# A conformer block: loads of the second batch's keys spread evenly over two query chunks, parked convolution chunks fetched one every second tick

## The chip, the cores and the metric

The kernel runs on one core of a Trainium2 chip. The metric is the device time of one execution in microseconds (us). The kernel is already tuned: TensorE is busy in 99% of the span.

## The reference, cut to what matters

```python
B, T, D = 2, 4000, 512
x1 = x + 0.5 * (silu(ln(x) @ w_ff1_a) @ w_ff1_b)
q, k, v = ln(x1) @ w_q, ln(x1) @ w_k, ln(x1) @ w_v
x2 = x1 + softmax(q @ k.T * D**-0.5) @ v @ w_o
a, b = split(ln(x2) @ w_pw1)                  # pointwise product ahead of the convolution
dc = depthwise_conv(a * sigmoid(b), taps=3)   # then normalised over all tokens
x3 = x2 + silu(norm(dc)) @ w_pw2
x4 = ln(x3 + 0.5 * (silu(ln(x3) @ w_ff2_a) @ w_ff2_b))
```

## The kernel before

Attention runs in 16 query chunks `g` (8 per batch element, 508 queries each, the last of a batch 444). A chunk has 32 ticks `kt`, one per tile of 128 keys. A tick is eight matmuls (four for the scores of the tile, four that weigh the values) and what a hook adds.

The keys of one batch element fill the buffers: `h` holds them as tokens by features, `hT` transposed. The second batch's keys may overwrite tile k once chunk 7 has used tile k, and chunk 8 needs it at its tick k.

```python
# attention(), at the end of every tick; KT = 32 key tiles, TCB = 8 chunks per batch
if not self.any_score:
    if g == TCB - 1 and kt >= 6:
        self.key_tile(1, kt - 6)
    if g == TCB and kt < 6:
        self.key_tile(1, KT - 6 + kt)
hook(g, kt)
self.tick()                       # runs jobs that were put off by so many ticks

def key_tile(self, b, kt):
    ...
    self.load(self.h[kt], src, [self.b_h[kt]], reads=rd)                  # plain load, issued by SP
    self.transpose(self.hT[kc][:, kj], src, rd, [self.b_hT[kc][kj]])      # transposing load, issued by SP
```

Convolution work of the chunk before is woven into attention. When the outputs of chunk g - 1 are projected, its tokens are normalised (VectorE), each of the four tiles is transposed by a transfer that SP issues as well (at ticks 16 and 17), and at tick 22 the pointwise product reads the four transposed tiles:

```python
def att_hook(g, kt):
    ...
    if kt in (22, 27) and (0 <= g - 1 < tail or ...):
        pair(g - 1, (22, 27).index(kt))            # conv_b: product with Wp1 (in "wff"), then conv_a
    ...
    if g == NCK - 1:                               # the last chunk, 15
        if kt >= 8 and kt % 4 == 0:
            for t in (kt // 4 - 2, TCB + kt // 4 - 2):
                if t < self.NBESIDE:
                    self.fetch_conv(t)             # a parked convolution chunk, 508 KB, back from HBM
```

Key loads, query tiles, those transposes, and stores of convolution chunks (`dcvd`) all pass through SP's queue one after the other (in the recorded profile two transposes whose input was ready by 955.4 us went out from 958.18, behind a key's transposing load that held SP for 1.19 us from 956.89).

## Time and profile before

| | |
|---|---|
| first three runs | 2052.74, 2054.47, 2055.17 us |
| the recorded profile's own run | 2051.23 us, span 2047.4 us |
| TensorE busy | 2029.9 us, 17.5 us idle |
| of it in chunk 7 | 3.50 us, one wait |
| of it in chunk 15 | 0.37 us, one wait |

The lines of the profile stand in the prediction below.

### The profile page before, as it was taken

How to read it: one execution, taken by the hardware profiler on the slowest of the kernel's cores; microseconds unless marked ns; L12 is line 12 of the kernel's file. 1: busy time of each engine (PE TensorE's matmuls, PEld its weight loads, DVE VectorE, ACT ScalarE, POOL GpSimd, SP SyncE). 2: the span in 40 equal slices, each digit the busy share in tenths (PEclk: the TensorE clock that was granted, in tenths of full speed). 3: DMA queues.
4: the chain of work that ended last, by engine and by line, in shares of the span. 5: the costliest groups of instructions: out<-in, count | busy, mean ns of one | idle time of the engine just before them, and what ended most of it. 6: DMA issues, size and time to landing. Idle time of an engine off the chain costs nothing.

```text
span 2047.4 us, 24513 instructions
## 1 busy us (share of the span) xinstructions
PE 2029.9 (99%) x9647; PEld 1028.7 (50%) x9649; DVE 1092.7 (53%) x2264; ACT 744.9 (36%) x1274; POOL 109.7 (5%) x236
## 2 busy tenths in 40 slices
PE   9999999999999999999999999999999999999998
PEld 5555555554444444444444444444445555555555
DVE  4244443334556667666766676667674434434434
ACT  3433333333333333333333333333345443433433
POOL 1000000000000000000000000000011000000000
PEclk9999999999999999999999999999999999999999
DMA  8222245420101011104411111011143111111111
GB/s 182 54 62 62 53 100 125 96 70 8 26 16 31 22 31 26 30 24 108 113 34 23 26 29 32 23 26 29 42 135 93 31 31 42 31 31 42 26 36 38
DMA packets 253120, 104.41 MB, mean 51 GB/s; under 512 B 193412, under 2 KB 252487, under 8 KB 252999
## 3 DMA queue, kind: packets, MB, share of 16 engines
q1 hardware_dynamic: 252751, 102.61, 21.2%
q8 instruction: 78, 1.28, 0.3%
q14 instruction: 43, 0.35, 0.1%
q10 hardware_dynamic: 248, 0.18, 0.0%
HBM read 33.77 MB, written 23.34 MB: 28 GB/s over the span
## 4 chain that ended last, share of the span: by engine, by line
PE 97%; DVE 1%; DMA 0%; SPq 0%; issue 0%; POOL 0%; ACT 0%; POOLq 0%; DVEq 0%; ACTq 0%
PE s L500 55%; PE y L500 42%; DVE wff L1176 0%; SPq L558 0%; DVE work L612 0%; DMA work<-work 0%; DMA wff<-in_w_ff_a_dram 0%; DVE xt L753 0%; SPq L562 0%; DVE work L634 0%; POOL work L726 0%; POOL work L1185 0%; ACT work L550 0%; DVE work L547 0%; SPq L554 0%
## 5 line engine op out<-in xcount | busy, mean ns | idle before, releaser
L550 ACT ACTIVATE work<-s 128x508 bf16<-128x508 f32 (+3 forms) x1060 | 622.8, 588 | 1211.9 <-PE s L500 1208.3
L500 PE MATMUL s<-work,wff 128*128 128x508 bf16 (+5 forms) x2624 | 628.3, 371 | 6.4 <-issue 3.5
L500 PE MATMUL s<-work,keys 128*128 128x508 bf16 (+1 forms) x2048 | 516.8, 374 | 0.1
L500 PE MATMUL y<-work,keys 128*128 128x508 bf16 (+2 forms) x2048 | 504.2, 373 | 0.4 <-DVE work L999 0.4
L500 PE MATMUL y<-wff,work 128*127 128x512 bf16 x1992 | 501.2, 379 | 0.0
L920 DVE TENSOR_TENSOR work<-work 128x508 f32<-128x508 f32 (+2 forms) x496 | 334.5, 674 | 279.8 <-ACT work L550 278.6
L500 PEld LDWEIGHTS s<-work,wff 128*128 128x128 bf16 x2624 | 252.2, 98 | 283.1 <-issue 10.1
L500 PEld LDWEIGHTS y<-wff,work 128*127 128x127 bf16 x1992 | 273.7, 137 | 171.4
L500 PEld LDWEIGHTS s<-work,keys 128*128 128x128 bf16 x2048 | 199.5, 98 | 231.9 <-issue 0.6
L500 PEld LDWEIGHTS y<-work,keys 128*128 128x128 bf16 (+1 forms) x2048 | 193.5, 97 | 234.0 <-issue 6.2
L753 DVE SCALAR_TENSOR_TENSOR xt<-y,xt 127x512 bf16<-127x512 f32 x126 | 78.5, 683 | 360.5 <-PE y L500 360.5
L612 DVE BATCH_NORM_STATS2 work<-xt 127x6 f32<-127x512 bf16 x312 | 197.2, 680 | 5.9 <-DMA xt<-in_x_dram 5.8
L500 PE MATMUL s<-work 128*127 128x512 bf16 (+3 forms) x776 | 197.0, 378 | 2.2 <-DVE work L1292 1.2
L621 POOL TENSOR_TENSOR work<-work 127x4 f32<-127x4 f32 (+1 forms) x76 | 76.7, 1009 | 1133.6 <-DVE work L619 1133.6
L500 PEld LDWEIGHTS s<-work 128*127 128x127 bf16 (+1 forms) x776 | 94.9, 124 | 77.0 <-issue 3.8
L634 DVE TENSOR_SCALAR work<-xt,work 127x512 bf16<-127x512 bf16 x307 | 110.7, 406 | 26.2 <-POOL work L621 23.0
L753 DVE SCALAR_TENSOR_TENSOR xt<-s,xt 127x512 bf16<-127x512 f32 x55 | 38.0, 692 | 144.6 <-PE s L500 144.6
L753 DVE SCALAR_TENSOR_TENSOR xt<-s,work,xt 127x512 bf16<-127x512 f32 x64 | 48.0, 750 | 30.8 <-PE s L500 30.2
L1074 DVE SCALAR_TENSOR_TENSOR wff<-wff,s 128x508 bf16<-128x508 f32 (+1 forms) x57 | 38.7, 678 | 45.3 <-PE s L500 45.1
L550 ACT ACTIVATE wff<-s 128x508 f32<-128x508 f32 (+1 forms) x67 | 39.5, 591 | 58.7 <-PE s L500 58.7
L550 ACT ACTIVATE work<-keys,work 128x508 bf16<-128x508 bf16 (+1 forms) x68 | 52.2, 774 | 1.4 <-DVE work L1190 1.3
L1155 POOL COPY wff<-wff 128x1 bf16<-128x1 bf16 x56 | 10.5, 188 | 638.8 <-DVE wff L1074 636.4
(83 smaller groups left out, 424.0 us busy)
## 6 DMA issues: line engine op xcount, KB each, us to landing
keys<-keysd SPq DMA_DIRECT2D x62, 128.0 KB, 2.3
keysd<-work SPq DMA_DIRECT2D x14, 448.0 KB, 3.2
out_dram<-work SPq DMA_DIRECT2D x14, 448.0 KB, 3.2
dcvd<-wff SPq DMA_DIRECT2D x48, 127.0 KB, 1.8
keys<-dcvd SPq DMA_DIRECT2D x12, 508.0 KB, 5.1
xt<-in_x_dram SPq DMA_DIRECT2D x13, 448.0 KB, 4.9
wff<-in_w_ff_a_dram SPq DMA_DIRECT2D x16, 256.0 KB, 6.3
work<-work SPq DMA_TRANSPOSE x208, 2.5
```

Of the source, the lines that this page charges most:

```text
L500: self.S.op("PE", lambda e: e.matmul(out, lhsT, rhs, start=start, stop=stop, **kw), reads=reads, writes=[bank], inc=stop if inc is None el ...
L550: return self.S.op("ACT", lambda e: e.activation(out, in_, func, **kw), reads=reads, writes=writes)
L612: self.S.op("DVE", lambda e: e.bn_stats(self.st[sl][:, ti, :], x), reads=[b_x], writes=[self.b_st[sl][ti]])
L621: S.op("POOL", lambda e: e.tensor_tensor(out=self.rs[sl][:, 0:n], in0=self.va[sl][:, 0:n], in1=self.neghalf[0:TILE, 0:n], op=ALU.pow), rea ...
L634: self.S.op("DVE", lambda e: e.tensor_scalar(out, x, self.mv[sl][:, ti, 0:1], self.rs[sl][:, ti:ti + 1], ALU.subtract, ALU.mult), reads=[b ...
L753: self.S.op("DVE", lambda e: e.scalar_tensor_tensor(out=self.XT[g][rows], in0=ps[rows], scalar=scalar, in1=self.XT[g][rows], op0=ALU.mult, ...
L920: S.op("DVE", lambda e, p=p, n=n, acc=acc: e.tensor_tensor(out=acc, in0=acc, in1=self.P[p][0:n, 0:W], op=ALU.add), reads=[self.b_P[p], sel ...
L1074: self.S.op("DVE", lambda e: e.scalar_tensor_tensor(out=out, in0=th, scalar=1.0, in1=ps[:, 0:W], op0=ALU.add, op1=ALU.mult), reads=[b_ps, ...
L1155: S.op("POOL", lambda e: e.tensor_copy(self.G[gs][:, jj, 0:1], self.G[gp][:, jj, CHUNK:CHUNK + 1]), reads=[self.b_G[gp][jj]], writes=[self ...
```

## The change

Its intent is to relieve the SP queue where it is fullest. Keys go out over both chunks that can take them, 32 keys in 52 ticks in place of 32; parked chunks go out singly in place of in pairs.

```diff
-                if not self.any_score:
-                    if g == TCB - 1 and kt >= 6:
-                        self.key_tile(1, kt - 6)
-                    if g == TCB and kt < 6:
-                        self.key_tile(1, KT - 6 + kt)
+                if not self.any_score and TCB - 1 <= g <= TCB:
+                    at = (g - TCB + 1) * KT + kt
+                    for k in range(KT):
+                        if 6 + k * (2 * KT - 12) // KT == at:
+                            self.key_tile(1, k)
...
-                if kt >= 8 and kt % 4 == 0:
-                    for t in (kt // 4 - 2, TCB + kt // 4 - 2):
-                        if t < self.NBESIDE:
-                            self.fetch_conv(t)
+                if kt >= 8 and kt % 2 == 0:
+                    t = kt // 4 - 2 + kt // 2 % 2 * TCB
+                    if t < self.NBESIDE:
+                        self.fetch_conv(t)
```

## The prediction

> **What bounds the kernel now.** I read the page top down: engine shares first, then the chain that ended last, then busy time per stretch, and only then single instructions. The first two say that TensorE is the bound all the way through.
>
> ```profile
> PE 2029.9 (99%) x9647; PEld 1028.7 (50%) x9649; DVE 1092.7 (53%) x2264; ACT 744.9 (36%) x1274; POOL 109.7 (5%) x236
> ...
> PE 97%; DVE 1%; DMA 0%; SPq 0%; issue 0%; POOL 0%; ACT 0%; POOLq 0%; DVEq 0%; ACTq 0%
> ```
>
> TensorE is busy 2029.9 us of 2047.4. All other engines together can give back at most the 17.5 us in which TensorE did nothing, and the change touches neither its instructions nor those of VectorE, ScalarE or GpSimd: set side by side, the two builds differ in order only on the SP queue, which issues the transfers. So I looked for the part of the 17.5 us that lies where the change works. It works in two stretches of attention: the last query chunk of the first batch and the first of the second (chunks 7 and 8), and the last chunk (15). I found the chunk borders in the chain in order of time, and asked for busy time in chunks 6, 7, 8, 9, then 14 and 15 (columns: stretch, length, busy us of each engine, clock, DMA share, GB/s):
>
> ```profile
> 857.00:924.50 67.50, 67.50 (x325) 31.46 (x322) 45.01 (x77) 23.21 (x41) 2.24 (x9) 1.00 0.12 28
> 924.50:990.10 65.60, 62.10 (x323) 31.37 (x322) 43.72 (x79) 21.91 (x41) 2.24 (x9) 1.00 0.52 119
> 990.10:1058.20 68.10, 68.10 (x337) 31.55 (x337) 45.02 (x77) 23.19 (x41) 2.31 (x11) 1.00 0.27 64
> 1058.20:1126.20 68.00, 68.00 (x341) 31.90 (x338) 44.79 (x77) 23.36 (x41) 1.90 (x9) 1.00 0.12 27
> 1399.50:1466.90 67.40, 67.40 (x321) 31.34 (x322) 45.89 (x81) 23.12 (x41) 2.23 (x9) 1.00 0.12 28
> 1466.90:1518.00 51.10, 50.73 (x268) 26.23 (x265) 39.72 (x88) 17.99 (x34) 2.29 (x7) 1.00 0.45 129
> ```
>
> The reader sees full stretches (busy equals length) everywhere but two: chunk 7 lost 65.60 - 62.10 = 3.50 us, and chunk 15 lost 51.10 - 50.73 = 0.37 us. Those are the two places that the change addresses, and together they are a fifth of all idle time of TensorE. The rest (start, and the convolution's tail after 1518 us) is out of its reach.
>
> **What the 3.5 us wait for.** The timeline of TensorE and of the SP queue around it:
>
> ```profile
> 962.56 0.91 PE L500 MATMUL y<-work,keys 128*128 128x444 bf16 x4
> 966.97 0.81 PE L500 MATMUL s<-work,wff 128*128 128x508 bf16 x3 [3.50 <-issue]
> ```
>
> ```profile
> 956.26 0.58 SPq L554 DMA_DIRECT2D keys<-keysd  x1
> 956.89 1.19 SPq L558 DMA_TRANSPOSE keys<-keysd  x1
> 958.18 2.89 SPq L558 DMA_TRANSPOSE work<-work  x2
> 961.12 0.57 SPq L554 DMA_DIRECT2D keys<-keysd  x1
> 961.74 1.19 SPq L558 DMA_TRANSPOSE keys<-keysd  x1
> 963.03 2.52 SPq L558 DMA_TRANSPOSE work<-work  x2
> ```
>
> The matmuls at 966.97 are the pointwise product that opens the convolution (they read wff, the convolution weights). They need four transposed tiles of normalised tokens: the four "work<-work" transposes. The page calls the releaser "issue", that is, it saw none; but the query on the transposes of this stretch lists "PE s L500: 3.5, 1" under those who waited for them, and the fourth is issued near 964.3 us and lands about 2.6 us later, which is 966.9. Their input was ready long before: VectorE's normalisations ran at 953.38 and 954.64 us, 0.73 us each pair, so done by 955.4. The transposes sat on the SP queue behind key loads. From 942 us on that queue shows no gap: each key costs it 0.58 + 1.19 us plus gaps, 1.86 us from key to key (950.70, 952.55, 954.41, 956.26), while a tick of this narrow chunk (444 columns, 8 matmuls) takes TensorE 1.50 us. One key per tick is more than the queue can issue, so it fell behind.
>
> [...] transposes whose inputs were ready at 955.4 stood behind key loads until 965.5. [...] a transpose holds SP for a median of 1.19 us against a landing time of 2.8 us, and in chunk 7 the issuing, not the DMA engines (52% busy), is what ran out. [...] the trace has four in 0.75 us, the same with DMA at 52% as in the quiet chunk 15; so transfer traffic does not slow TensorE, and only stalls can be won.
>
> **The change, part by part.** It adds and removes no work: the same 32 keys (a plain load and a transposing load each) and 13 parked chunks.
>
> *Keys.* Before, key k is queued at tick 6 + k of chunk 7. After, at tick 6 + 1.625 k rounded down, counted over both chunks' 64 ticks: 16 keys in each chunk. The transposes for the convolution are queued at ticks 16 and 17 of the chunk, the product at tick 22. Ahead of the first pair stood keys 0 to 10, eleven of them; now keys 0 to 6, seven. Four keys less are 4 x 1.86 = 7.4 us less on SP, so the queue is through its keys at 958.1 - 7.4, about 951, and idles until the normalisations. Then I estimate: first transpose at about 953.8 (its input), second ends at 956.3, one key between the pairs as before (to 958.1), the third to 959.4, the fourth issued at 959.4 and landed 2.6 us later: 962.0. TensorE would arrive at 962.56 + 4 x 0.1875 = 963.31. The wait vanishes with some 1.3 us to spare. Worth: next start 966.97 instead of 963.31, **3.66 us** (the 3.50 of the page plus the pipeline's overlap).
>
> *Chunk 8, which receives 16 keys in place of 6.* Its ticks are about 2.1 us, a key comes every 1.625 ticks, 3.4 us, against 1.86 us of queue: no backlog. The four transposes there ran from 1022.42 to 1027.54, the last issued at 1026.26; one key between them moves it to 1028.1, landed by 1031, while the product starts at 1033.38. Key 31 is queued at tick 24, wanted at tick 31, some 15 us later, against 5 us to issue and land: no wait. The query tiles for chunk 9 were issued late, 1008.19 to 1013.3, by the old backlog; they get earlier. Cost 0.
>
> *Parked chunks.* Two every fourth tick become one every second. Five instead of six precede chunk 15's transposes, but SP had nothing to do between 1493.2 and the first transpose at 1496.20: that one waited for VectorE (normalisation at 1495.76). The fourth lands about 1502.6 as before, so this 0.37 us stays. Later ones (last fetched at tick 28 in both) are wanted only in the tail. Worth: 0, at most 0.2.
>
> *Sum:* 2054.47 - 3.66 = **2050.8 us**, a ratio of 0.998.
>
> **Rivals.** (1) The transfers are hidden anyway: time unchanged at 2054.5. For it: 97% of the chain is TensorE. Against it: the 3.50 us in chunk 7 are TensorE's own idle time, and no later slack exists to swallow them, as chunks 8 to 14 are full. (2) A new wait replaces the old: keys arriving late for chunk 8, since the last has 7 ticks of lead instead of 25, or SP blocked in order behind a store that waits for VectorE (the list of SP waits has "SPq L567 <- DVE wff L1112", longest 13.9 us). A late key could cost a few us, giving 2054 to 2058. Against it: in chunk 8 such stores are queued near ticks 7, 12 and 27, the first two far from the need of any key and the third after the last key. (3) The transposes still land late, because landing times reach 3.9 us in this stretch: the margin of 1.3 us would turn into a remainder of at most 1 us, 2051.8. (4) Bunched transfers slow matmuls, and smoothing them wins more: then chunk 7 and 15 would show wider spacing than quiet chunks. They do not.
>
> **Range and chances.** The three runs of before span 2.4 us, and its profiled run gave 2051.23, so chance alone moves a median by some 1 to 1.5 us. The mechanism puts the gain between 2.5 and 4.2 us; with run noise on both sides that makes 2048.5 to 2053.5. Faster by over 2% would need 41 us, more than twice all TensorE idle time; slower by 2% would need a stall that nothing here feeds. So 0.99 for the same.
>
> **What would show it.** Right: chunk 7 has TensorE busy equal to its length, the bracket "[3.50 <-issue]" is gone, SP shows gaps before the "work<-work" transposes, chunk 8's DMA share rises from 0.27 to nearly chunk 7's, both near 0.4, and chunk 15 still has about 0.4 us of idle before its product. The chunk after the stall starts 3.7 us sooner, and so does everything behind it. Wrong: a new idle before a score matmul in chunk 8 (a late key), or idle of over 1 us left at the same product, or a gap elsewhere. A median above 2053.5 with a clean chunk 7 would mean that the tail lost what the middle won.

The sum came to 2050.8 us with a gain of 3.66 us. The 0.1875 us per matmul in it is a quarter of the 0.75 us that the trace shows for four.

## The result, and the profile after

The changed kernel takes 2047.21 us (median of 4 runs, 2046.86 to 2047.44) against 2053.88 us (4 runs). The ratio is 0.9967, with a 95% interval of 0.995 to 0.9984. Ratios here are the mean time of one kernel's fast runs over that of the other's of the same rounds, so not quite the ratio of the medians. The gain is 6.7 us by medians, near twice the 3.66 us predicted, and 2047.21 lies below the range's lower end of 2048.5.

Yet the trace shows just what was foretold. First busy time of the engines on the page of the changed kernel, then its chunks 7, 8 and 15 (stretch, length, busy us of PE, PEld, DVE, ACT, POOL, then the TensorE clock that was granted, 1.00 being full speed, the mean busy share of the 16 DMA engines, and GB/s):

```profile
PE 2029.6 (99%) x9649; PEld 1028.9 (50%) x9649; DVE 1093.0 (54%) x2264; ACT 743.9 (36%) x1274; POOL 109.4 (5%) x236
```

```profile
923.70:985.60 61.90, 61.90 (x325) 31.39 (x322) 43.73 (x79) 21.83 (x41) 2.23 (x9) 1.00 0.42 98
985.60:1053.70 68.10, 68.10 (x340) 31.54 (x336) 45.06 (x77) 23.16 (x41) 2.30 (x11) 1.00 0.37 90
1462.40:1513.60 51.20, 50.84 (x269) 26.28 (x266) 39.74 (x88) 18.07 (x34) 2.29 (x7) 1.00 0.43 128
```

Chunk 7 is full now (61.90 of 61.90), chunk 8 stays full though it took over keys, and chunk 15 keeps its 0.36 us. The timeline of TensorE and of SP around the product of chunk 7 in the changed kernel:

```profile
961.77 0.91 PE L500 MATMUL y<-work,keys 128*128 128x444 bf16 x4
962.52 0.81 PE L500 MATMUL s<-work,wff 128*128 128x508 bf16 x3
```

```profile
949.21 1.19 SPq L558 DMA_TRANSPOSE keys<-keysd  x1
953.03 2.50 SPq L558 DMA_TRANSPOSE work<-work  x2
955.58 0.58 SPq L554 DMA_DIRECT2D keys<-keysd  x1
956.20 1.20 SPq L558 DMA_TRANSPOSE keys<-keysd  x1
957.49 3.30 SPq L558 DMA_TRANSPOSE work<-work  x2
```

The product follows at once, without a bracket (which gives the idle time just before a group, and what ended it). SP has nothing to do from 950.40 to 953.03, then issues the first pair of transposes as soon as their input is there (VectorE normalises the first tile from 952.60, in 0.41 us). The span fell by 4.3 us (2047.4 to 2043.1): 3.66 us here and 0.79 us at the start, 4.45 together, of which some 0.1 us is lost again behind the last matmuls. At the start TensorE waits for the first tokens and weights, for a time that differs from run to run in both kernels (its first long group after that wait began at 11.91 us before and 11.12 us after).

So the two traces differ by 4.3 us and the medians by 6.7 us. The profiled run of the changed kernel took 2046.86 us, like all its runs; that of before took 2051.23 us, 2.65 us under its median. Something made most runs of before slower than the one that had been looked at.

### The profile page after: what moved, and what is told of

Same layout as the page of the kernel before. It is cut to its first block, busy times and chain, and to the rows that moved or that the text cites. A ratio compares the mean times of both kernels' runs of the same rounds, so it can differ in the third digit from the quotient of the medians.

```text
span 2043.1 us, 24518 instructions
## 1 busy us (share of the span) xinstructions
PE 2029.6 (99%) x9649; PEld 1028.9 (50%) x9649; DVE 1093.0 (54%) x2264; ACT 743.9 (36%) x1274; POOL 109.4 (5%) x236
## 4 chain that ended last, share of the span: by engine, by line
PE 97%; DVE 1%; issue 0%; POOL 0%; DMA 0%; ACT 0%; POOLq 0%; SPq 0%; DVEq 0%; ACTq 0%
PE s L500 55%; PE y L500 42%; DVE work L612 0%; DVE wff L1177 0%; POOL work L726 0%; ACT work L550 0%; DVE xt L753 0%; DMA work<-work 0%; DMA xt<-in_x_dram 0%; DVE work L634 0%; POOL work L1186 0%; DVE work L547 0%; DVE wff L1071 0%; DVE work L920 0%; DVE work L719 0%
```

## The experiments

**The same two kernels again, and each half of the change alone.** Theory 1: the wait in chunk 7 costs more in most runs than in the recorded profile. Rivals: an offset of chip or session (2), a variation elsewhere (3), or the parked chunks bring the rest. All four ran on one chip, with 9 runs of before (median 2053.17 us); the later groups of experiments ran on two other chips, each again with 9 runs of before (medians 2053.45 and 2053.41 us).

The kernel before, unchanged:

> The kernel before, unchanged, timed against itself and profiled again. The recorded before profile lasted 2051.23 us, its other runs 2052.74 to 2055.17; the change gained 6.7 us by medians where the two profiles differ by 4.3 us (3.66 us in chunk 7, 0.79 us at the start). Theory 1 (the chunk 7 wait varies from run to run and was short in the recorded profile): times scatter over 2 us or more, and the new profile shows the idle before the chunk 7 product at 3.5 to 7 us, longer when the run is longer. Theory 2 (the recorded profile was of another chip or session, an offset that both kernels share): times here near 2051 with little scatter, the wait 3.5 us again. Theory 3 (a varying wait elsewhere, for example for the first weights): the wait stays 3.5 us and another idle stretch is 1 to 3 us longer.

Measured: 2052.97 us median, 2051.14 to 2054.06, ratio 0.9995. Theory 2 falls: before is near 2053 here too. Theory 1 holds, but not in the form in which I had put it: the wait is only 0.6 us longer. Its timeline of TensorE, then three stretches of 3.41 us (columns as above; the third number from the right is the clock):

```profile
961.91 0.91 PE L500 MATMUL y<-work,keys 128*128 128x444 bf16 x4
966.91 3.38 PE L500 MATMUL s<-work,wff 128*128 128x508 bf16 x8 [4.09 <-issue]
```

```profile
963.18:966.59 3.41, 0.00 (x0) 0.00 (x0) 0.12 (x1) 0.00 (x0) 0.00 (x0) 1.00 0.54 112
966.59:970.00 3.41, 3.09 (x8) 1.18 (x9) 0.00 (x0) 0.59 (x1) 0.00 (x0) 0.50 0.56 146
970.00:973.40 3.40, 3.40 (x20) 1.73 (x18) 1.56 (x3) 1.08 (x2) 0.30 (x2) 1.00 0.55 138
```

The reader sees a second cost. After the wait the granted clock is 0.50 for 3.41 us: eight matmuls take 3.38 us, where they take 1.89 us at full speed. In that stretch TensorE starts 8 matmuls; at full speed, by my estimate, it would have started some 15 in the same time (the product's 8 and 7 of the attention's: in the recorded profile the 8 take 1.72 us from start to start, and each four of the attention's 0.75 us). The recorded profile of before, in stretches of the same length around its wait:

```profile
961.55:964.96 3.41, 1.92 (x11) 0.78 (x8) 1.24 (x2) 0.79 (x2) 0.00 (x0) 1.00 0.62 142
964.96:968.38 3.42, 1.41 (x7) 0.71 (x8) 0.00 (x0) 0.35 (x1) 0.00 (x0) 1.00 0.48 110
968.38:971.79 3.41, 3.41 (x20) 1.75 (x18) 1.38 (x3) 1.32 (x3) 0.31 (x2) 1.00 0.58 140
```

There the wait was 3.66 us and the clock stayed at 1.00. Why it fell in the one run and not in the other is not shown by these traces.

The keys half alone:

```diff
-                    if g == TCB - 1 and kt >= 6:
-                        self.key_tile(1, kt - 6)
-                    ...
+                        if 6 + k * (2 * KT - 12) // KT == at:
+                            self.key_tile(1, k)
```

> The keys part of the change alone. If the whole gain is the chunk 7 wait (theory 1 or 3): same time as the full change, 2047.2 us within 0.5, TensorE without idle in chunk 7, chunk 15 idle 0.37 us. If the parked chunks carry the 2.8 us that the prediction missed: about 2050.

Measured: 2047.70 us (2046.95 to 2048.14), ratio 0.9971. Its chunk 7:

```profile
924.00:986.00 62.00, 62.00 (x322) 31.45 (x322) 43.73 (x79) 21.93 (x41) 2.22 (x9) 1.00 0.43 97
```

The parked chunks alone:

```diff
-                if kt >= 8 and kt % 4 == 0:
-                    for t in (kt // 4 - 2, TCB + kt // 4 - 2):
-                    ...
+                if kt >= 8 and kt % 2 == 0:
+                    t = kt // 4 - 2 + kt // 2 % 2 * TCB
```

> The parked chunks part alone. If it is worth nothing, as predicted: equal to the kernel before within its scatter, about 2053.5, the chunk 7 idle still there, the chunk 15 idle 0.37 us. If it carries the missing part: some 2.8 us faster, about 2051.

Measured: 2053.33 us, ratio 0.9999. Its chunk 7, with idle time and with a mean clock of 0.98:

```profile
925.20:993.50 68.30, 64.09 (x324) 31.89 (x322) 44.04 (x80) 22.27 (x42) 2.24 (x9) 0.98 0.50 120
```

The keys are the gain; the parked chunks are worth nothing that shows above the scatter of the runs.

The changed kernel again:

> The changed kernel, unchanged, beside the others on this chip. Theory 1: 2047.2 us within 0.5 and a scatter under 1 us, as the wait that varied is gone, while before scatters by 2 us or more. Theory 2 (offset of a chip or session): before and after differ by 3.7 us only, on this chip. Theory 3 (variation elsewhere): after scatters as much as before.

Measured: 2047.19 us (2046.76 to 2048.05), ratio 0.9968. It scatters by 1.3 us (under 1 us was expected), before by 2.9 us in the same rounds. The gain by medians of the same rounds is 5.98 us.

**Keep the clock up, keep the wait.** If the halved clock is a cause of its own, filling the wait with useless work must make the kernel faster, though every transfer stays where it was.

```diff
+            if g == TCB - 1 and kt == 22 and not any_score:
+                ps, b_ps = self.sbank()
+                for _ in range(12):
+                    self.mm(ps[:, :], self.ident, self.Wvo[:, 0, :], True, True, [self.b_ident, self.b_Wvo], b_ps)
             if kt in (22, 27) and ...:
                 pair(g - 1, (22, 27).index(kt))
```

> The kernel before plus twelve dummy matmuls of 512 columns (2.6 us) directly ahead of the product that waits in chunk 7; no transfer is moved. Clock theory (TensorE idles about 4 us there, and in most runs its granted clock then falls to half for 3.4 us, which costs 1.7 us more; the recorded before profile was one of the few without): the idle is cut to 1.0 to 1.8 us, the clock record shows no half-speed stretch near 965 us, the product starts at the same time as before, and the kernel with MORE work is 1.0 to 1.7 us faster than before, near 2051.5. Rival (the clock is not the cause, the scatter is a longer queue delay): no gain, 2053.2, and half-speed stretches remain or do not matter.

Measured: 2051.36 us (2050.93 to 2051.98) against 2053.45 us of before in the same rounds, 2.09 us faster by medians. The interval of the ratio, 0.9976 to 1.0003, just includes 1, so by that measure the times alone do not settle it, though each of the five runs lies under each of the nine of before (2052.39 us and up). The trace shows the cause:

```profile
963.56 2.54 PE L500 MATMUL s<-work 128*128 128x512 bf16 x11
967.16 1.02 PE L500 MATMUL s<-work,wff 128*128 128x508 bf16 x4 [1.06 <-issue]
```

The dummies (one of the twelve has no record in the trace) fill the wait down to 1.06 us, the product still starts at 967.16, and four of its matmuls take 1.02 us, full speed. The clock record of this run has no half-speed stretch between the start and the end (1.00 from 930 to 974.4 us, 1.000 as the mean of the run). The gain by medians is a little over the 1.0 to 1.7 us expected; in one profile further below the half speed lasts for 6.83 us, which the expectation had not allowed for.

**Issue time or traffic?** The prediction put the late transposes down to SP's time for issuing, not to the DMA engines. Two experiments move one without the other. First, ScalarE's queue issues the plain loads of the second batch's keys: same bytes, same ticks, less work for SP.

```diff
-        self.load(self.h[kt], src, [self.b_h[kt]], reads=rd)
+        self.load(self.h[kt], src, [self.b_h[kt]], reads=rd, eng="ACT" if b else "SP")
```

> The kernel before with one key per tick, only that the plain loads of the second batch's keys are issued by ScalarE's queue; SP keeps the transposing ones (1.24 us per key in place of 1.86). Same bytes at the same ticks. Issue theory (the queue's issue time made the transposes late): chunk 7 without idle, 2047.2 us within 0.7, like the full change. Traffic theory (the DMA engines were busy with bunched keys): the idle stays at 3 us or more, and 2052 to 2054.

Measured: 2048.38 us (four runs, 2048.31 to 2048.44), ratio 0.9975. Chunk 7, and SP's queue in it:

```profile
924.60:986.50 61.90, 61.85 (x324) 31.29 (x320) 43.71 (x79) 21.70 (x40) 2.23 (x9) 1.00 0.68 141
```

```profile
946.88 6.44 SPq L558 DMA_TRANSPOSE keys<-keysd  x5
954.06 2.50 SPq L558 DMA_TRANSPOSE work<-work  x2
```

The wait is gone with one key per tick, while the DMA share of the chunk is higher than before (0.68 against 0.52). Traffic was not the cause. The time is 1.2 us above the changed kernel, outside the 0.7 that I had allowed. In the profiled run 0.98 us of this lie at the very start, where the first long group begins at 12.10 us in place of 11.12. The edit does not touch the start, and the second profile of the changed kernel (after_again, 2048.05 us) begins it at 12.11, so a start of this length is no mark of the edit. The other three runs have no trace, and why all four lie within 0.13 us of each other stays open.

Second, each plain key load in two halves: same bytes, one issue more per key.

```diff
-        self.load(self.h[kt], src, [self.b_h[kt]], reads=rd)
+        halves = ((0, 64), (64, 128)) if b else ((0, 128),)
+        self.S.dma("SP", self.S.dsems[self.nxt("ld", 16)],
+                   *[lambda e, lo=lo, hi=hi: e.dma_start(self.h[kt][lo:hi], src[lo:hi]) for lo, hi in halves],
+                   reads=rd, writes=[self.b_h[kt]])
```

> The kernel before with each plain key load of the second batch issued as two halves (64 partitions each): same bytes, one issue more per key. Issue theory: eleven keys ahead of the transposes cost 11 x 0.6 = 6.6 us more, plus one between the pairs, so the idle grows from 4 to about 10 to 11.5 us and the time to about 2059 to 2061 (the clock falls in any case, its cost of 1.7 us stays). Traffic theory: the same bytes give the same idle, 2053.

Measured: 2074.55 us (2073.89 to 2077.1), ratio 1.0105. The direction is that of the issue theory; the size is beyond what it foretold. TensorE in chunks 7 and 8:

```profile
975.59 3.55 PE L500 MATMUL s<-work,wff 128*128 128x508 bf16 x8 [12.01 <-DMA work<-work]
```

```profile
1021.20 1.85 PE L500 MATMUL s<-work,keys 128*128 128x508 bf16 x4 [5.00 <-DVE xt L753]
1038.21 1.01 PE L500 MATMUL s<-work 128*128 128x508 bf16 x2 [5.00 <-DMA work<-keysd]
```

The idle in chunk 7 grew to 12.0 us (10 to 11.5 expected; a key now holds SP for some 2.58 us in place of 1.86). The DMA engines were no busier for it (0.37 over 924 to 991 us). What I had left out are two waits of 5.00 us in chunk 8: the backlog reached on to the transposes of the softmax sums, which VectorE needs for the residuals, and to the query tiles. Each of the three waits came with a stretch at half speed, of 13.65, 3.41 and 3.41 us (the mean clock was 0.90 over 924 to 991 us and 0.95 over 991 to 1060).

**More profiles of the kernel before.**

> The kernel before once more, for one more profile of the same program. Clock theory: either a half-speed stretch of 3.4 us right after the idle and 2053 us or more, or none and about 2051. Rival: time and half-speed stretch have nothing to do with each other.

Measured: 2053.11 us. Half speed from 967.62 to 971.03 us, just behind the wait, which ended at 967.02.

```profile
967.02 3.00 PE L500 MATMUL s<-work,wff 128*128 128x508 bf16 x8 [3.59 <-issue]
```

```profile
964.20:967.62 3.42, 0.60 (x3) 0.32 (x4) 0.00 (x0) 0.00 (x0) 0.00 (x0) 1.00 0.52 115
967.62:971.03 3.41, 3.41 (x10) 1.29 (x9) 0.69 (x1) 0.59 (x1) 0.14 (x2) 0.50 0.56 143
```

> The kernel before, one more profile. Window theory: the clock falls [...] in the chunk 7 idle, [...] So either [...] and about 2051, or [...], half speed for 3.4 us and 2052.5 or more.

Measured: 2053.84 us. Its stretches of 3.41 us, columns as above:

```profile
962.22:965.63 3.41, 0.61 (x4) 0.10 (x1) 0.62 (x1) 0.44 (x1) 0.00 (x0) 1.00 0.59 129
965.63:969.05 3.42, 2.50 (x7) 0.89 (x8) 0.00 (x0) 0.59 (x1) 0.00 (x0) 0.50 0.48 123
969.05:972.46 3.41, 3.41 (x10) 1.34 (x9) 0.96 (x2) 0.54 (x1) 0.30 (x2) 0.50 0.62 149
972.46:975.90 3.44, 3.44 (x20) 1.80 (x19) 2.02 (x4) 1.08 (x2) 0.00 (x0) 1.00 0.52 129
```

Here the clock fell inside the wait, at 965.63, 0.92 us before the product started at 966.55, and half speed lasted until 972.46: 6.83 us, twice as long as in before_again.

With these the time of each profiled run of a kernel with bunched keys can be taken apart. The wait is the start of the product less the start of the four matmuls ahead of it less their 0.75 us (for before_again 966.91 - 961.91 - 0.75 = 4.25). The clock's cost is an estimate: half of the time that TensorE worked at half speed (970.00 - 966.91 = 3.09, so 1.55), since the product's eight matmuls took 3.38 us there and 1.89 us at full speed.

| profiled run | time, us | wait | clock | time less both |
|---|---|---|---|---|
| before, as recorded | 2051.23 | 3.66 | 0 | 2047.57 |
| before_again | 2053.07 | 4.25 | 1.55 | 2047.27 |
| before_third | 2053.11 | 3.75 | 1.71 | 2047.65 |
| before_fourth | 2053.84 | 3.88 | 2.95 | 2047.01 |
| conv_only | 2054.05 | 4.37 | 1.68 | 2048.00 |

The last column lies within the changed kernel's own runs, 2046.76 to 2048.05 us. Wait and clock are the whole difference, to within the scatter of the changed kernel. The other runs with such waits close as well, worked the same way: fill with 2047.55 (wait 3.81, no half speed), gap, which is shown below, with 2047.23 (3.78 and 1.68), and split_loads with 2047.61 (22.49 in three waits, and 4.74). What scatter is left is the start: the last column of the table less the time at which the first long group begins (11.91, 11.26, 11.87, 11.27 and 12.10 us) is 2035.7 to 2036.0 in all five rows, and 2035.7 and 2035.9 in the two profiles of the changed kernel (11.12 and 12.11).

The executions without a trace bear this out, as the record lists the mean granted clock of each. The profiled ones of before with a half-speed stretch have 0.998, the recorded one without has 1.000. Of the 32 executions of before in the rounds of these experiments, 24 have 0.998 (median 2053.55 us), two have 1.000 (2051.85 and 2052.32 us), and six have 0.999, which the rounding leaves open. No execution of the changed kernel, keys_only, act_loads, fill or best has 0.998.

Part of the wait's own variation is a single issue: the transposing load of key 1 held SP for 1.87 us in the recorded profile and for 2.37 us in before_again, and the issues behind it shifted.

**Would fewer keys ahead of the transposes have been enough?** One key per tick as before, but none at ticks 13 to 17 of chunk 7; then one per tick again, to tick 10 of chunk 8.

```diff
+                if not self.any_score and TCB - 1 <= g <= TCB:
+                    at = (g - TCB + 1) * KT + kt
+                    k = at - 6 if at < 13 else at - 11 if at >= 18 else -1
+                    if 0 <= k < KT:
+                        self.key_tile(1, k)
```

> One key per tick as before, but none at ticks 13 to 17 of chunk 7, so that seven keys stand ahead of the convolution's transposes, as in the change; afterwards one per tick again, to tick 10 of chunk 8. Queue theory: the chunk 7 idle and its half-speed clock are gone, but SP is still overfull behind: it idles 3 us before the transposes and TensorE is 5 to 6 us earlier, so the query tiles for chunk 9 land late, and a new idle of 3 to 7 us opens at their product in chunk 8 (tick 14); about 2051 to 2056. If only the number of keys ahead of the transposes matters: 2047.2 like the change.

Measured: 2053.89 us, ratio 1.0003: nothing gained. TensorE's idle in chunk 8, and the busy times of chunk 7 and of the stretch with that wait:

```profile
1015.76 1.85 PE L500 MATMUL s<-work 128*128 128x508 bf16 x4 [3.63 <-issue]
```

```profile
924.00:987.00 63.00, 63.00 (x329) 31.92 (x326) 44.35 (x81) 22.94 (x43) 2.22 (x9) 1.00 0.47 110
987.00:1015.00 28.00, 25.13 (x116) 11.46 (x114) 21.41 (x39) 7.81 (x14) 1.61 (x5) 1.00 0.56 133
```

Chunk 7 is full, and a wait of the same size opens at the product of the query tiles, as expected, with half speed from 1015.72 to 1019.13 (the mean clock was 0.96 over 1015 to 1056 us). Holding back five keys (those of ticks 13 to 17) for the transposes only moved the lateness; the spread over both chunks took it away.

**A version on top of the change.** Chunk 15's small wait remains in the changed kernel. Here its product goes one tick later:

```diff
-            if kt in (22, 27) and (... (22, 27).index(kt) < self.KEEP):
-                pair(g - 1, (22, 27).index(kt))
+            late = g == NCK - 1
+            if kt in (22 + late, 27) and (... (22 + late, 27).index(kt) < self.KEEP):
+                pair(g - 1, (22 + late, 27).index(kt))
```

> The changed kernel plus one thing: in chunk 15 the convolution product moves from tick 22 to tick 23, as its fourth transpose lands about 0.5 us after TensorE would start it. Expected: the idle of 0.37 us there is gone and nothing else moves, 2046.7 us, 0.5 less than the changed kernel (within the scatter of its start, so the trace decides).

Measured: 2046.88 us (2046.41 to 2047.15), ratio 0.9968. Its chunk 15:

```profile
1462.00:1513.00 51.00, 51.00 (x270) 26.27 (x269) 39.82 (x89) 17.99 (x34) 2.29 (x7) 1.00 0.45 130
```

The wait is gone. The median is the lowest of all, but 0.3 us under the changed kernel's is less than the scatter of the runs, so as a time it is not shown to be faster than the change.

## Why the prediction was right or wrong

- **Right: where and why.** The wait in chunk 7, SP's issue time as its cause and the number of keys ahead as the lever are shown by keys_only, act_loads and split_loads. Chunk 8 stayed full, the DMA shares of chunks 7 and 8 became 0.42 and 0.37 ("both near 0.4"), the parked chunks gave nothing, chunk 15 kept its wait.
- **Wrong: the step "Worth", a term of the sum that was too small.** The prediction said "Worth: next start 966.97 instead of 963.31, **3.66 us**". That was the wait alone, as one execution had it, and the sum took it from the median of other executions. In four of the five profiles with bunched keys the wait was followed by TensorE at half speed. Over the four profiles of before the wait is 3.9 us and the clock costs 1.55 us on average, 5.4 us together; by medians of the same rounds the gain is 5.98 us. The remaining half microsecond is of the size of the scatter at the start; in runs without a trace it can't be followed.
- **The sign that was passed over.** "The three runs of before span 2.4 us, and its profiled run gave 2051.23, so chance alone moves a median by some 1 to 1.5 us." This took the scatter for chance. A profiled run 3.2 us below the median of the others says that the profile shows a better case than the one being predicted; from 2051.23 the same 3.66 us would have given 2047.6. And the range left out the clock's fall, which that profile, with its clock at 1.00 through the wait, does not show.
- **Also off, without effect: the margin of "some 1.3 us".** In the changed kernel the second pair's transposes took 3.3 to 3.8 us to land, not 2.6, and one of them held SP for 2.04 us. The last landed at 962.05, half a microsecond before the product started at 962.52. The change just fits.
- **Two readings that are looser than they look.** That transposes "stood behind key loads until 965.5" shows the order of the queue, not a wait of SP for their input; such a wait shows in the changed kernel, where SP does nothing from 950.40 to 953.03 until the normalised tokens are there. And chunk 15 is not quiet as a whole (DMA share 0.45); its first ticks are (0.01 from 1467 to 1475 us), and there four matmuls take 0.75 us too, so the reading stands.
- **The rivals.** None of the four came about in the changed kernel: no late key, no remainder, and matmul spacing was the same with bunched and with spread transfers (four matmuls of 444 columns in 0.75 us, from 961.81 before and from 961.77 after).

## What to carry to other kernels

Before a wait of TensorE is priced, compare the profiled run's time with the median of the others. Of the nine waits of 3.6 us and more that these traces show unfilled, eight brought a half-speed stretch with them, and the ninth was the one in the run that was profiled first: count on the stretch (it cost an estimated 1.55 to 2.95 us in chunk 7), and don't trust one trace to show it. Count what an issuing queue must issue per tick, not only bytes (here 1.86 us of SP for a key, in a tick of 1.50 us). The overfull queue handed its lateness to whatever stood behind it (in gap a wait of 3.63 us in chunk 8 for the one gone from chunk 7), so spread the load until the backlog is gone rather than around one victim.
